# Weight forms of a two-layer MLP made in the first token pass and read back in the second, with VectorE and GpSimd work in another order

## The chip, the cores and the metric

One core of a Trainium2 chip runs the whole program. The metric is the time of one execution in device microseconds, as the median of several runs. A profile of one execution gives the times within it.

## The reference

Of 2048 tokens with 576 features, a spectral filter and then an MLP are computed, each on the layer-normed input and added to it. The biases and scales of the norms are absent.

```python
h  = x + irfft2(rfft2(layernorm(x)) * (w_r + 1j * w_i), s=(2048, 576))
h2 = h + relu(layernorm(h) @ w1) @ w2      # w1: 576 x 4608, w2: 4608 x 576
```

Everything is float32, inputs and output alike.

## The kernel before

**Front part.** The two Fourier transforms are products with constant cosine and sine matrices. The loop over `t` at the end of the listing carries their last stage (`inv_d`, `inv_a`), the second layer norm (`stat2`, `norm2`), and `project`, which transposes the normed tokens for the MLP. Its last seven turns (`t` from 16 to 22) also run block 0 of the MLP.

**Exact products from halves.** TensorE multiplies operands of type fp32r. To keep float32 accuracy each operand v is split in a high half (ScalarE copies v, rounded to fp32r) and a low half (VectorE subtracts the high half from v). A product then is three: high x high, high x low, low x high. `split` does this everywhere. Such a pair of halves is called a form here.

**Seven products for eight.** Both layers use the Strassen-Winograd scheme: of a 2x2 arrangement of blocks seven products are made, from sums of the blocks. The sums on the weights' side are GpSimd's (`sums1` for the first layer: S1 to S4 and one for the rest of 64 features; `sums2` for the second: T1 to T4), the sums on the side of the activations (`hsum`) and the final additions VectorE's.

**Blocks and slots.** The 4608 hidden features are handled as 9 blocks of 512, and the tokens in two passes of 1024: block s = 0 to 8 is the first token pass, s = 9 to 17 the second, with the same weights in the same order (`v % 18`, `s % 9`). A block has two units u = 0 and 1 of 256 hidden features; unit v = 2s + u. A block takes 14 slots k, seven to a unit (m = k % 7). A slot S, k holds on TensorE 6 or 8 matmuls of the first layer for block S (`mm1`, product m) and 12 of the second layer for block S-1 (`prod`, product k of `PRODS`). After the last block there are 14 slots with second-layer products alone. `evac` takes the first layer's result from the PSUM banks X and Y: ScalarE copies X (products 0, 2, 4), VectorE adds Y to such a copy (products 1, 4, 6) into `h`, ScalarE applies relu. Products 1 and 3 both begin in Y, so product 3 waits for the addition of product 1. `form` makes the form of a second-layer operand two slots ahead of its use.

**Order.** Nothing is scheduled automatically: the order in which the Python code issues instructions is each engine's order. In a slot that is `form`, `mm1`, `evac`, `prod` with its addition to the output tile `xs`, then `tasks_old` (work for block S-1) and `tasks_new` (for block S and the next unit). All DMAs of the MLP stand in one queue, SP's; a DMA that waits for a buffer holds back all behind it.

**Weight forms and buffers.** `load1` brings a unit's 576 x 256 weights to one of two buffers `V1`; `sums1` fills `SW` (one buffer); `split1` makes the forms in `WF` in four groups: 0 (A11, A12 and part of the rest; 5 columns of 128), 1 (A22 and rest; 3), 2 (S1, S2; 4), 3 (S3, S4 and the rest's difference; 5). `WF` exists once and a group is overwritten as soon as TensorE has used it. Group 0 is used in products 0 and 1, group 2 in 2 and 3, group 3 in 4 and 6, group 1 in 3 and 5. `load2` brings the second layer's four blocks B11 to B22 to `V2`, T1 to T4 are made in their place or in `T2`, and `split2` makes the seven forms in a ring of four buffers `VF`. `load1`, `load2`, `sums1`, `split1`, `sums2` and `split2` run in each of the 18 blocks.

For the second pass the transposed tokens go through DRAM: `project` writes them to `Td` from seven buffers `h`, and the last seven slots of block 8 read them back into `T` (line 624).

Of the kernel before, what the change touches and what calls it, by code (L numbers as in the profile page):

```python
# [21 lines left out]
NS = 18  # L22
WARM = 60
# [101 lines left out]
def kernel(ctx: ExitStack, tc: tile.TileContext, x, w_r, w_i, w1, w2, cc2, c1, fb, ib, c3, out):  # L125
# [244 lines left out]
    Td = dram.tile([7, 128, 4, 4, 128], F32, tag="Td", name="Td")  # L370
    for k in range(8):
        load_x(xs, 2 * k, 2)
# [52 lines left out]
    def project(i, part):  # L425
# [11 lines left out]
        if P == 0:  # L437
            dsts = [(0, nf, T[:, f0:f0 + nf, :, :, q])]
        else:
            dsts = [(a, b, sb([128, 2, 2, 2, 128], "h", 7, F32R, "mid")[:, :b - a]) for a, b in ((0, 2), (2, nf))]  # L440
        for a, b, dst in dsts:
            act(dst[:, :, 0], pv[:, a:b])
            nc.vector.tensor_sub(dst[:, :, 1], pv[:, a:b], dst[:, :, 0])
        if part == 0:
            rp = pz[64:128, 768:].rearrange("p (c n) -> p c n", c=2)
            act(R[P][64:128, :, q], rp)
            nc.vector.tensor_sub(R[P][0:64, :, q], rp, R[P][64:128, :, q])
        if P:
            for a, b, dst in dsts:
                for f in range(a, b):  # L450
                    nc.sync.dma_start(Td[f0 + f, :, :, i % 4], dst[:, f - a].rearrange("p h k n -> p (h k) n").bitcast(F32))
# [10 lines left out]
    V1, V2, VF, HF, hr = [], {}, [], [], {}  # L462
    M = {}

# [4 lines left out]
    def load1(v):  # L469
        t, f = V1[v % 2], slice(256 * (v % 18), 256 * (v % 18) + 256)  # L470
# [4 lines left out]
    def sums1(v, part, only=None):  # L475
        t, S = V1[v % 2], M["SW"]
# [3 lines left out]
        for n_ in ((0, 1), (2, 3, 4))[part] if only is None else [only]:  # L480
            (nc.gpsimd.tensor_sub if n_ else nc.gpsimd.tensor_add)(*ops[n_])  # L481

    def split1(v, g):
        t, S = V1[v % 2], M["SW"]
        a, b, src = ((0, 5, t[:, :, :128]), (5, 8, t[:, 2:5, 128:]), (8, 12, S[:, 0:4]), (12, 17, S[:, 4:9]))[g]
        split(WF[:, 0, a:b], WF[:, 1, a:b], src)

    def load2(s, n_):
        u, h = int(n_[1]) - 1, int(n_[2]) - 1
        f = 512 * (s % 9) + 256 * u  # L490
        nc.sync.dma_start(V2[n_], w2[f:f + 256, 288 * h:288 * h + 288].rearrange("(j p) d -> p j d", p=128))

    def sums2(*names):
        o = {"T1": ("B11", "B12", "B11"), "T3": ("B12", "B22", "B12"), "T2": ("T2", "B22", "B11"), "T4": ("B21", "B21", "T2")}
        for n_ in names:
            d, a, b = (V2[x] for x in o[n_])
            nc.gpsimd.tensor_sub(d, a, b)  # L497
# [6 lines left out]
    def split2(s, n_):  # L504
        f = vform(s, n_)
        split(f[:, 0], f[:, 1], V2[PLACE.get(n_, n_)])

    def raw(s, q, j=slice(0, 2)):
        if (s, q) not in hr:
            hr[s, q] = sb([128, 2, 512], "h", 7, pool="mid")  # L510
# [44 lines left out]
    def prod(s, k):  # L555
# [6 lines left out]
        for tt in range(2):  # L562
            ops = [(l, r, j) for j in range(2) for l, r in ((0, 0), (0, 1), (1, 0))]
            for n_, (l, r, j) in enumerate(ops):
                nc.tensor.matmul(o[:, tt], f[:, l, j, 128 * tt:128 * tt + 128], w[:, r, j], start=first and n_ == 0,  # L565
                                 stop=n_ == 5, skip_group_check=not first)
        t0 = 8 * (s // 9) + c + 4 * x
# [7 lines left out]
    def tasks_old(s, k):  # L575
        if k == 0:
            hsum(s, "S1", 0)
            hsum(s, "S2", 1)
        if k == 1:
            hsum(s, "S2", 0)  # L580
            split2(s, "T2")
        if k == 2:
            hsum(s, "S4", 0)
        if k == 3:
            split2(s, "T1")
            hsum(s, "S4", 1)
        if k == 4:
            sums2("T4")
        if k == 5:
            split2(s, "B22")  # L590
            split2(s, "T3")
        if k == 8:
            split2(s, "T4")

    def tasks_new(s, k):
        u, m = divmod(k, 7)
        v = 2 * s + u
        if k == 9:
            hsum(s, "S3")
        if k == 11:  # L600
            split2(s, "B11")
            sums2("T1", "T2", "T3")
        if k == 12:
            split2(s, "B21")
        if k == 13:
            hsum(s, "S1", 1)
        if v and k == 7:
            split1(v, 1)
        if v and k in (2, 7):
            split1(v, 3)  # L610
        if m == 0 and v + 2 < 2 * NS:
            load1(v + 2)
        if v + 1 < 2 * NS:
            if v and k in (3, 5, 9, 12):
                sums1(v + 1, int(k in (5, 12)))
            if k in (4, 6, 10, 12, 13):
                split1(v + 1, {4: 0, 6: 2, 10: 0, 12: 2, 13: 1}[k])
        if s:
# [104 lines left out]
```

## Time and profile before

| | |
|---|---|
| median of 3 runs | 1078.07 us (1077.25 to 1078.86) |
| profiled execution | 1077.19 us, span 1075.4 us, granted TensorE clock 0.99 |
| instructions | 16681 |
| block 0 with the last transposes | from about 195 to 240 us |
| blocks 1 to 17 | from about 240 to 1043 us |
| second-layer products alone | from 1043 us |
| DRAM read and written | 71.98 MB and 12.06 MB |

The profile has the columns of the engines: PE is TensorE's matmul, PEld its weight load (which overlaps), DVE VectorE, ACT ScalarE, POOL GpSimd, SP the queue of the DMAs. A row such as `L539 PE MATMUL X<-T,WF` names line, engine, operation, and output and inputs by the program's names; buffer numbers are left out, and `e` is the pool of ten buffers that hold `V1`, `SW`, `V2`, most of `VF` and one of the second-layer operands. `d` are PSUM tiles, `A` is the output tile `xs`, `h` the first layer's result. L467 is the low half in `split`, whichever form it makes, L161 the high half and other ScalarE copies, L516 a sum of activations, L552 the addition of bank Y, L565 the second layer's matmul, L570 the addition to the output, L481 and L497 GpSimd's sums of the first and second layer, L423 its sums for `project`.

### The profile page before, as it was taken

The numbers are of one execution on the slowest core, as the hardware profiler recorded it, in microseconds if no ns is written. First come the engines' busy times: TensorE is split into PE (matmuls) and PEld (weight loads), VectorE is DVE, ScalarE is ACT, GpSimd is POOL, SyncE is SP. The second block draws the span as 40 slices with busy tenths as digits, with TensorE's granted clock in tenths as the row PEclk, the third lists the DMA queues.
The fourth block names the chain that finished last, engine by engine and source line by source line (L and its number), as shares of the span: only waits on it lengthen the run. The fifth ranks groups of instructions, "written<-read, shape, count | busy, mean of one in ns | idle before, by whom it ended". The sixth has DMA issues, their size and how long they took to land.

```text
span 1075.4 us, 16681 instructions
## 1 busy us (share of the span) xinstructions
PE 1011.2 (94%) x6344; PEld 887.4 (83%) x6344; DVE 921.2 (86%) x1367; ACT 514.9 (48%) x904; POOL 368.4 (34%) x384
## 2 busy tenths in 40 slices
PE   8999598779999999999999999999999999999997
PEld 7788476659988988888888989888898988888896
DVE  7587478679899898989989898998989898998987
ACT  4533133556464545545454544545454554545442
POOL 4200166453424252342425235242523424251420
PEclk9999899999999999999999999999999999999999
DMA  8850900563121212112121744212121121212013
GB/s 235 198 133 2 225 1 1 146 183 97 53 67 35 69 36 58 58 44 75 36 69 36 265 147 103 82 36 69 36 58 49 46 82 38 69 30 64 15 31 89
DMA packets 73936, 85.13 MB, mean 79 GB/s; under 512 B 5248, under 2 KB 69248, under 8 KB 72960
## 3 DMA queue, kind: packets, MB, share of 16 engines
q1 hardware_dynamic: 73856, 84.06, 27.7%
q8 instruction: 50, 0.82, 0.3%
q14 instruction: 30, 0.25, 0.1%
HBM read 71.98 MB, written 12.06 MB: 78 GB/s over the span
## 4 chain that ended last, share of the span: by engine, by line
PE 56%; DVE 30%; ACT 7%; issue 3%; DMA 2%; POOL 2%; SPq 1%; POOLq 0%; DVEq 0%; ACTq 0%
PE d L565 22%; PE X L539 15%; PE Y L539 9%; PE d L158 6%; DVE WF L467 6%; DVE e L467 5%; DVE A L570 4%; DVE G L467 3%; DVE h L516 3%; PE dd L158 2%; DVE HF L467 2%; DVE h L552 2%; ACT e L161 1%; ACT WF L161 1%; DVE st L220 1%
## 5 line engine op out<-in xcount | busy, mean ns | idle before, releaser
L539 PE MATMUL X<-T,WF 128*128 128x512 f32 x864 | 230.4, 399 | 12.1 <-DVE WF L467 8.8
L570 DVE TENSOR_TENSOR A<-A,d 128x576 f32<-128x576 f32 x252 | 188.2, 747 | 41.5 <-PE d L565 41.3
L565 PEld LDWEIGHTS d<-e,G 128*128 128x128 f32 x1512 | 213.7, 188 | 11.8 <-issue 1.4
L565 PE MATMUL d<-e,G 128*128 128x288 f32 x1512 | 221.2, 295 | 1.2 <-DVE A L570 1.0
L553 ACT ACTIVATE h<-h 128x512 f32<-128x512 f32 x108 | 68.3, 633 | 315.1 <-DVE h L552 314.7
L481 POOL TENSOR_TENSOR e<-e 128x256 f32<-128x256 f32 (+1 forms) x108 | 98.2, 916 | 300.0 <-DVE WF L467 289.2
L539 PEld LDWEIGHTS X<-T,WF 128*128 128x128 f32 x864 | 154.8, 190 | 44.5 <-DVE WF L467 15.8
L539 PE MATMUL Y<-T,WF 128*128 128x512 f32 x648 | 169.0, 396 | 15.5 <-DVE h L552 15.5
L467 DVE TENSOR_TENSOR WF<-e,WF 128x640 fp32r<-128x640 f32 (+2 forms) x144 | 142.4, 1000 | 32.5 <-ACT WF L161 32.5
L539 PEld LDWEIGHTS Y<-T,WF 128*128 128x128 f32 x648 | 115.4, 188 | 38.6 <-DVE h L552 19.5
L565 PEld LDWEIGHTS d<-e,e 128*128 128x128 f32 x756 | 106.9, 188 | 7.4 <-issue 1.8
L565 PE MATMUL d<-e,e 128*128 128x288 f32 x756 | 110.9, 295 | 1.8 <-DVE A L570 1.6
L565 PEld LDWEIGHTS d<-e,HF 128*128 128x128 f32 x756 | 107.7, 189 | 5.3
L565 PE MATMUL d<-e,HF 128*128 128x288 f32 x756 | 111.2, 296 | 0.0
L497 POOL TENSOR_TENSOR e<-e 128x576 f32<-128x576 f32 x18 | 32.3, 1796 | 229.6 <-DVE e L467 216.9
L467 DVE TENSOR_TENSOR e<-e,e 128x576 fp32r<-128x576 f32 x108 | 96.6, 908 | 15.7 <-ACT e L161 14.4
L516 DVE TENSOR_TENSOR h<-h,h 128x512 f32<-128x512 f32 (+1 forms) x126 | 109.8, 882 | 0.0
L467 DVE TENSOR_TENSOR G<-h,G 128x512 fp32r<-128x512 f32 x126 | 103.6, 823 | 0.1
L161 ACT ACTIVATE WF<-e 128x640 fp32r<-128x640 f32 (+2 forms) x144 | 91.0, 645 | 9.1 <-POOL e L481 9.1
L481 POOL TENSOR_TENSOR e<-e,e 128x256 f32<-128x256 f32 x72 | 82.0, 1139 | 2.8
L161 ACT ACTIVATE u<-X 128x512 f32<-128x512 f32 x72 | 42.5, 590 | 82.4 <-PE X L539 82.3
L161 ACT ACTIVATE G<-h 128x512 fp32r<-128x512 f32 x126 | 77.8, 619 | 6.5 <-DVE h L516 3.5
(103 smaller groups left out, 1296.4 us busy)
## 6 DMA issues: line engine op xcount, KB each, us to landing
e<-in_B_w_dram SPq DMA_DIRECT2D x72, 288.0 KB, 2.9
e<-in_B_w_dram SPq DMA_DIRECT2D x36, 512.0 KB, 3.7
Td<-h SPq DMA_DIRECT2D x28, 256.0 KB, 3.0
T<-Td SPq DMA_DIRECT2D x7, 1024.0 KB, 8.8
A<-in_A_x_dram SPq DMA_DIRECT2D x16, 288.0 KB, 9.2
e<-in_B_w_dram SPq DMA_DIRECT2D x72, 64.0 KB, 3.4
out_dram<-A SPq DMA_DIRECT2D x32, 144.0 KB, 2.5
X<-in_A_x_dram SPq DMA_DIRECT2D x12, 288.0 KB, 7.7
```

The lines of the kernel that those rows point to most:

```text
L158: nc.tensor.matmul(o, l, r, start=start, stop=stop)
L161: nc.scalar.activation(o, i, AF.Copy, **kw)
L220: nc.vector.bn_stats(st[:, i, h, :], xs[:, t0 + i, 288 * h:288 * h + 288])
L467: nc.vector.tensor_sub(l, v, h)
L481: (nc.gpsimd.tensor_sub if n_ else nc.gpsimd.tensor_add)(*ops[n_])
L497: nc.gpsimd.tensor_sub(d, a, b)
L516: f(raw(s, d, j), raw(s, a, j), raw(s, b, j))
L539: nc.tensor.matmul(o, l, r, start=first and n_ == 0, stop=n_ == len(ops) - 1, skip_group_check=not first)
L552: nc.vector.tensor_add(h, a, Y)
L553: nc.scalar.activation(h, h, AF.Relu)
L565: nc.tensor.matmul(o[:, tt], f[:, l, j, 128 * tt:128 * tt + 128], w[:, r, j], start=first and n_ == 0, stop=n_ == 5, skip_group_check=not ...
L570: nc.vector.tensor_add(xt, xt, o)
```

## The change

- Blocks 0 to 9 make the forms as before; block 9, the first of the second pass, works on the same 512 features as block 8, and blocks 10 to 17 on those of blocks 0 to 7 (`fblock`, `made`). In blocks 0 to 7 each form is written to DRAM (`WFd`, `VFd`) right after its split. Blocks 10 to 17 read the forms back into the same places, and have no loads, sums or splits of weights.
- GpSimd's sums stand one to a slot: a unit's five first-layer sums in slots 2 to 6 for the odd unit and 7 to 9, 0, 1 for the even one, T1 to T4 in slots 10 to 13. `SW` has two buffers.
- VectorE's order in a slot is another: `S2` and `S4` are whole sums instead of two halves, the splits of the second layer stand in slots 10, 12, 13 and 3, 4, 5, 7, and the addition to the output (now `total`) comes before the new tasks in odd slots and last in even ones.
- `load1` stands in a unit's third slot instead of its first, and each `load2` right behind the split that frees its buffer.
- `project` writes from four buffers `HF` that later hold the second-layer operands, and issues each write right behind its split. `h` has six buffers.

```diff
-            dsts = [(a, b, sb([128, 2, 2, 2, 128], "h", 7, F32R, "mid")[:, :b - a]) for a, b in ((0, 2), (2, nf))]
+            dsts = [(0, 2, None), (2, nf, None)]
         for a, b, dst in dsts:
+            if P:
+                dst = sb([128, 2, 2, 2, 128], "HF", 4, F32R, "mid")[:, :b - a]
             act(dst[:, :, 0], pv[:, a:b])
             nc.vector.tensor_sub(dst[:, :, 1], pv[:, a:b], dst[:, :, 0])
+            for f in range(a, b) if P else ():
+                nc.sync.dma_start(Td[f0 + f, :, :, i % 4], ...)
...
+    def fblock(s):
+        return s if s < 9 else 8 if s == 9 else s - 10
+
+    def made(s):
+        return s < 10
...
+    GROUPS = ((0, 5), (5, 8), (8, 12), (12, 17))
+
+    def copy1(v, g, back):
+        a, b = GROUPS[g]
+        w, d = WF[:, :, a:b].rearrange("p h a f -> p h (a f)").bitcast(F32), WFd[(v - 20 * back), :, :, 128 * a:128 * b]
+        nc.sync.dma_start(*((w, d) if back else (d, w)))
...
+        if v < 2 * NK1:
+            copy1(v, g, False)
...
+    def copy2(s, n_, back):
+        w, d = vform(s, n_).rearrange("p a j d -> p (a j d)").bitcast(F32), VFd[s - 10 * back, VORDER.index(n_)]
+        nc.sync.dma_start(*((w, d) if back else (d, w)))
...
     def tasks_old(s, k):
         if k == 0:
             hsum(s, "S1", 0)
-            hsum(s, "S2", 1)
         if k == 1:
-            hsum(s, "S2", 0)
-            split2(s, "T2")
+            hsum(s, "S2")
+
+    def tasks_late(s, k):
         if k == 2:
-            hsum(s, "S4", 0)
...
+            hsum(s, "S4")
+        for kk, n_ in ((3, "T1"), (4, "T3"), (5, "B22"), (7, "T4")) if made(s) else ():
+            if k == kk:
+                split2(s, n_)
+        for kk, n_ in ((0, "T1"), (3, "B22"), (4, "T3"), (7, "T4")) if not made(s) else ():
+            if k == kk:
+                copy2(s, n_, True)
...
+        if made(s):
+            if v and m == 0:
+                split1(v, 1)
+            if v and m == 2 - u:
+                split1(v, 3)
+        elif m == 0:
+            copy1(v, 3, True)
...
+            if made((v + 1) // 2):
+                if m == 5 - 2 * u:
+                    split1(v + 1, 0)
+                if m == 6 - 2 * u:
+                    split1(v + 1, 2)
+            else:
+                for mm_, g in ((2, 0), (4, 2), (6, 1)):
+                    if m == mm_:
+                        copy1(v + 1, g, True)
+        if made(s):
+            for kk, n_ in ((10, "B11"), (12, "B21"), (13, "T2")):
+                if k == kk and (s or kk < 13):
+                    split2(s, n_)
+        else:
+            for kk, n_ in ((10, "B11"), (11, "T2"), (12, "B21")):
+                if k == kk:
+                    copy2(s, n_, True)
...
-        if m == 0 and v + 2 < 2 * NS:
+        if 2 <= k < 7 and made(s):
+            sum1(2 * s + 1, k - 2)
+        if 7 <= k < 10 and made(s + 1):
+            sum1(2 * s + 2, k - 7)
+        if k < 2 and s and made(s):
+            sum1(2 * s, k + 3)
+        if m == 2 and made((v + 2) // 2):
             load1(v + 2)
...
+        if made(s):
+            if 10 <= k < 14 and (s or k < 13):
+                sum2("T" + "1234"[k - 10])
+            for kk, n_ in ((4, "B11"), (5, "B12"), (6, "B22"), (8, "B21")) if s else ():
                 if k == kk:
                     load2(s, n_)
...
+            if k % 2:
+                total(S - 1, k)
         if S < NS:
             tasks_new(S, k)
+        if S:
+            tasks_late(S - 1, k)
+            if k % 2 == 0:
+                total(S - 1, k)
```

In the program as built the change shows first on VectorE, which TensorE waits for in slots 3 and 4. These are its instructions from the end of slot 0 to slot 2 in a block of the first pass, before. `HF`, `e<-h` and `G` rows are low halves of second-layer operands, `e<-T` that of T2, the L552 row is the addition that frees Y, and the two `WF` rows are weight groups; the last row is group 3:

```order
L516 TENSOR_TENSOR h_3128<-h_3128,h_3326 128x512
L516 TENSOR_TENSOR h_3047<-h_3128,h_3047 128x512
L467 TENSOR_TENSOR e_2112<-h_3247,e_2112 128x512
L552 TENSOR_TENSOR h_3443<-s_296_1847,Y 128x512
L570 TENSOR_TENSOR A_1284<-A_1284,d_2217 128x2x288
L516 TENSOR_TENSOR h_3047<-h_3128,h_3047 128x512
L467 TENSOR_TENSOR e_2213<-T_300_1857,e_2213 128x576
L467 TENSOR_TENSOR G_2214<-h_3047,G_2214 128x512
L570 TENSOR_TENSOR A_1284<-A_1284,d_2216 128x2x288
L516 TENSOR_TENSOR h_3247<-h_3247,h_3047 128x512
L467 TENSOR_TENSOR WF_1288<-e_1323,WF_1288 128x640
```

The same slots in the change (from slot 0's sum on), where L476 is the low half of `split`, L539 the sum of activations, L575 the addition of Y and L599 the addition to the output:

```order
L539 TENSOR_TENSOR h_3173<-h_3173,h_3383 128x512
L476 TENSOR_TENSOR WF_1288<-e_1321,WF_1288 128x384
L599 TENSOR_TENSOR A_1284<-A_1284,d_2231 128x2x288
L476 TENSOR_TENSOR HF_2175<-h_3295,HF_2175 128x512
L575 TENSOR_TENSOR h_3498<-s_297_1849,Y 128x512
L539 TENSOR_TENSOR h_3089<-h_3173,h_3089 128x1024
L599 TENSOR_TENSOR A_1284<-A_1284,d_2233 128x2x288
L476 TENSOR_TENSOR HF_2229<-h_3089,HF_2229 128x512
L476 TENSOR_TENSOR WF_1288<-e_1325,WF_1288 128x640
L539 TENSOR_TENSOR h_3295<-h_3295,h_3089 128x1024
```

The split of T2 has left the place, the half sums have become one, and the sum S4 stands behind the weight group instead of ahead of it.

The second place is ScalarE at the start of block 1, where the last piece of `project` meets the first second-layer operands. Before (`h_339`, `h_340` are the pieces, `G_343` the operands, `s1` the copy of bank X for product 0):

```order
L161 ACTIVATE h_339_2202<-d_338_2193 128x2x256
L161 ACTIVATE h_340_2203<-d_338_2193 128x2x256
L161 ACTIVATE G_343_2214<-h_302_1887 128x512
L161 ACTIVATE s1_296_1847<-X_1854 128x512
L161 ACTIVATE G_343_2214<-h_326_2074 128x512
```

And now, where `HF_340` and `HF_344` are the same memory, and so are `HF_341` and `HF_345`:

```order
L162 ACTIVATE HF_340_2213<-d_339_2204 128x2x256
L162 ACTIVATE HF_341_2218<-d_339_2204 128x2x256
L162 ACTIVATE e_342_2223<-V_300_1858 128x576
L162 ACTIVATE HF_344_2229<-h_302_1885 128x512
L162 ACTIVATE s1_297_1849<-X_1856 128x512
L162 ACTIVATE WF_202_1288<-e_205_1321 128x384
L162 ACTIVATE HF_345_2230<-h_325_2078 128x512
```

The operand for slot 2 now has to wait until the piece has been written to DRAM, and the copy of bank X stands behind it.

The third place is SP's queue in a block of the first pass. Before it held loads alone (L491 the second layer's, L471 and L473 the first's):

```order
L491 DMA e_1958<-in_B_w_dram 128x2x288
L491 DMA e_1961<-in_B_w_dram 128x2x288
L491 DMA e_1958<-in_B_w_dram 128x2x288
L471 DMA e_1359<-in_B_w_dram 128x4x256
L473 DMA e_1359<-in_B_w_dram 64x256 x2
L491 DMA e_1961<-in_B_w_dram 128x2x288
```

And now (`WFd` and `VFd` are the forms in DRAM, L509 the second layer's loads):

```order
L518 DMA VFd<-e_2223 128x1152
L509 DMA e_1911<-in_B_w_dram 128x2x288
L518 DMA VFd<-e_2121 128x1152
L497 DMA WFd<-WF_1288 256x1x640
L509 DMA e_1911<-in_B_w_dram 128x2x288
L518 DMA VFd<-e_2224 128x1152
L497 DMA WFd<-WF_1288 256x1x512
L509 DMA e_1964<-in_B_w_dram 128x2x288
L497 DMA WFd<-WF_1288 256x1x384
L518 DMA VFd<-e_2173 128x1152
```

The loads of the second layer's weights stand between the copies that write the forms out.

More of the change, by code (lines that the diff above doesn't have):

```diff
@@ L473, in load1, with sum1 @@
             nc.sync.dma_start(t[64 * h:64 * h + 64, 4], w1[512:576, f])
-    def sums1(v, part, only=None):
-        t, S = V1[v % 2], M["SW"]
+    def sum1(v, n_):
+        t, S = V1[v % 2], SW[v % 2]
         A11, A12, A21, A22 = (t[:, 2 * k:2 * k + 2, 128 * f:128 * f + 128] for f, k in ((0, 0), (0, 1), (1, 0), (1, 1)))
```

106 lines of the change are left out of this document (42 added, 64 removed).

## The prediction

> **What bounds the kernel now.** I read the page's busy line first, then a table of stretches of the span, the timeline of TensorE, the chain and the waits. The busy line:
>
> ```profile
> PE 1011.2 (94%) x6344; PEld 887.4 (83%) x6344; DVE 921.2 (86%) x1367; ACT 514.9 (48%) x904; POOL 368.4 (34%) x384
> ```
>
> TensorE and VectorE are both near full, so the share alone doesn't say which one sets the pace. The stretches do (columns: busy time of TensorE, its weight loads, VectorE, ScalarE and GpSimd, then granted clock, DMA share, GB/s):
>
> ```profile
> 250.40:297.00 46.60, 46.60 (x279) 42.32 (x278) 41.54 (x55) 23.42 (x43) 15.96 (x14) 1.00 0.22 66
> ...
> 723.00:770.30 47.30, 45.99 (x268) 40.96 (x268) 42.91 (x57) 23.80 (x43) 16.85 (x14) 1.00 0.18 54
> ...
> 581.10:628.40 47.30, 45.98 (x268) 40.97 (x268) 42.91 (x57) 23.80 (x43) 16.85 (x14) 1.00 0.57 209
> ...
> 1045.00:1075.40 30.40, 22.60 (x158) 21.01 (x156) 24.55 (x38) 10.31 (x18) 0.70 (x1) 0.97 0.33 78
> ```
>
> In the first stretch (block 1) TensorE has no gap at all and its clock is 1.00. In the later blocks about 1.3 us of each 47.30 is a gap. The timeline of TensorE shows where; in brackets stands the idle time before a row and what ended it:
>
> ```profile
> 251.68 1.53 PE L539 MATMUL Y<-T,WF 128*128 128x512 f32 x6
> ...
> 297.86 1.66 PE L539 MATMUL Y<-T,WF 128*128 128x512 f32 x6 [0.86 <-DVE h L552]
> ...
> 723.03 1.66 PE L539 MATMUL Y<-T,WF 128*128 128x512 f32 x6 [0.76 <-DVE h L552]
> ...
> 727.75 1.20 PE L539 MATMUL X<-T,WF 128*128 128x512 f32 x4 [0.55 <-DVE WF L467]
> ...
> 1006.66 1.65 PE L539 MATMUL Y<-T,WF 128*128 128x512 f32 x6 [0.77 <-DVE h L552]
> ...
> 1043.44 3.36 PE L565 MATMUL d<-e,G 128*128 128x288 f32 x24
> ...
> 1050.19 1.83 PE L565 MATMUL d<-e,e 128*128 128x288 f32 x12 [1.63 <-DVE A L570]
> ...
> 1067.31 3.36 PE L565 MATMUL d<-e,G 128*128 128x288 f32 x24
> ```
>
> The same two waits come once in each block: slot 3 waits for VectorE's sum of slot 1 (line 552), which frees bank Y, and slot 4 for the low half of the fourth weight group. The first is the start of a block's slot 3, at 251.68 in block 1 and at 1006.66 in block 17: 754.98 us for 16 blocks, 47.19 us each.
>
> How long would a block take without them? The chain gives the pace of an undisturbed TensorE:
>
> ```profile
> 699.55 1.86 PE Y L539 x8
> 701.40 1.59 PE d L565 x12
> 703.00 1.40 PE X L539 x6
> ```
>
> A block has 14 slots. Eight have 8 matmuls of the first layer (1.86), six have 6 (1.40), and each has 12 of the second (1.59): 14.88 + 8.40 + 22.26 = 45.54 us. Block 1 is a second measure: from 251.68 to 297.86 less the wait of 0.86 and about 0.15 by which a modelled end overstates is 45.17 us. I take 45.4. So TensorE's own floor is 1.8 us below today's pace, and that is nearly all that the steady part has to give.
>
> VectorE is late because GpSimd works in bursts. First rows of VectorE, then of GpSimd, then how far two shapes of VectorE's instruction spread (min/median/max ns):
>
> ```profile
> 711.73 1.92 DVE L467 TENSOR_TENSOR WF<-e,WF 128x512 fp32r<-128x512 f32 x1
> ...
> 717.99 1.92 DVE L467 TENSOR_TENSOR G<-h,G 128x512 fp32r<-128x512 f32 x1
> ...
> 726.88 0.82 DVE L467 TENSOR_TENSOR WF<-e,WF 128x640 fp32r<-128x640 f32 x1
> ```
>
> ```profile
> 707.86 1.82 POOL L497 TENSOR_TENSOR e<-e 128x576 f32<-128x576 f32 x1 [12.71 <-DVE e L467]
> ...
> 711.14 1.95 POOL L497 TENSOR_TENSOR e<-e,e 128x576 f32<-128x576 f32 x1
> ...
> 717.62 1.75 POOL L497 TENSOR_TENSOR e<-e,T 128x576 f32<-128x576 f32 x1
> ```
>
> ```profile
> L467 DVE TENSOR_TENSOR G<-h,G x126: 677/684/1921, 246.2 to 1066.7; 128x512 fp32r<-128x512 f32 x126
> ...
> L570 DVE TENSOR_TENSOR A<-A,d x252: 737/746/756, 246.8 to 1070.7; 128x576 f32<-128x576 f32 x126
> ```
>
> The VectorE instruction begun at 711.73 ends at 713.65, 0.56 after GpSimd's at 713.09; the one at 717.99 ends at 719.91, 0.54 after GpSimd's. A difference of two SBUF operands does nothing until GpSimd's instruction is over, and then takes its usual time. Mean less median over the split and sum groups comes to 5.9 us a block, against 16.85 us of GpSimd work. Eight sums stand in a row from 707.9 to 719.4, just ahead of both late instructions.
>
> **The change, part by part.** *Second token pass (blocks 10 to 17).* Gone are 64 splits of the first layer's weights, 56 of the second's, and 112 GpSimd sums. Rows:
>
> ```profile
> L467 DVE TENSOR_TENSOR WF<-e,WF 128x640 fp32r<-128x640 f32 (+2 forms) x144 | 142.4, 1000 | 32.5 <-ACT WF L161 32.5
> ...
> L467 DVE TENSOR_TENSOR e<-e,e 128x576 fp32r<-128x576 f32 x108 | 96.6, 908 | 15.7 <-ACT e L161 14.4
> ...
> L516 DVE TENSOR_TENSOR h<-h,h 128x512 f32<-128x512 f32 x108 | 87.8, 826 | 0.0
> ...
> L516 DVE TENSOR_TENSOR h<-h,h 128x1024 f32<-128x1024 f32 x18 | 21.9, 1219 | 0.0
> ```
>
> Per block 8 x 1.00 + 7 x 0.908 = 14.4 us leave VectorE, which falls from 42.9 to about 28.5. It can't be late any more; TensorE sets 45.4. Gain 8 x 1.79 = 14.3 us.
>
> In their place SP issues 8 reads of weight forms of layer 1 and 7 of layer 2 a block. WF has one buffer of four groups, so a group is read again only when TensorE has used it. The tightest are the second layer's B21, free at the start of slot 12 and wanted in slot 1 of the next block (3.45 + 3.45 + 2.99 + 1.86 = 11.7 us later), and the groups of A22 and S3/S4, with 12.9. The nearest rows (KB, median us from issue to landing), and what the DMA engines moved from 615 to 650, with the reload of T in its first quarter:
>
> ```profile
> e<-in_B_w_dram SPq DMA_DIRECT2D x36, 512.0 KB, 3.7
> Td<-h SPq DMA_DIRECT2D x28, 256.0 KB, 3.0
> T<-Td SPq DMA_DIRECT2D x7, 1024.0 KB, 8.8
> ```
>
> ```profile
> GB/s 421 440 431 440 421 403 412 421 243 47 4 156 373 214 2 0 0 82 215 50 0 0 0 80 227 153 215 19 0 0 0 22 234 360 58 0 0 36 224 153
> ```
>
> A copy of 0.4 to 0.66 MB therefore lands between 3.0 and 8.8 us after its issue, under 11.7 at either end; I cost it at nothing. 8.6 MB a block in 45.4 us is 190 GB/s, under half of the 421 to 440. The block with the reload (581.10, 209 GB/s, share 0.57) has the same 47.30 us and the same busy times as the others, so traffic doesn't slow the engines.
>
> *First pass (blocks 2 to 9).* All splits and sums stay, 36 pairs of half sums become whole (4 x 0.826 - 2 x 1.219 = 0.87 us less a block), and each form is also written out: 2 x 2.23 + 7 x 0.59 = 8.6 MB more a block in blocks 1 to 7. With today's 2.4 that is 11 MB, 242 GB/s, a good half of what the reload reached. WF groups and second-layer buffers are overwritten five or more slots after the copy is issued, over 15 us against 3.0 to 8.8: nothing. The first layer's loads move from a unit's first slot to its third; they are wanted five slots later (16 us) and land in 3.7. SP used to stand still for the weights of layer 2:
>
> ```profile
> SPq L491 <- DVE e L467: 329.8, 65, 30.2
> ```
>
> Copies behind such a wait would be late, but loads now stand right behind the split that frees their buffer, so the queue follows the program. VectorE's load is 42.0 us of 45.4 if collisions cost what they do now. What counts is that no instruction needed by slots 3 and 4 is behind a burst. T2's split no longer stands ahead of the fourth group's, the pairs of half sums have become whole, and each slot meets one GpSimd instruction. Slots 1 to 3 hold 3.3, 3.5 and 2.2 us without collisions (splits at 0.68 to 0.82, a sum of 1024 columns 1.22, an addition to the output 0.75), 9.0 of TensorE's 9.9, and the split in slot 2 has until slot 4. I leave 0.2 us a block for waits that remain. Gain 8 x 1.59 = 12.7 us.
>
> *End.* Slots 4 to 13 of block 17 lose the second wait, 0.7 us. From 1043.44 the last 14 slots have second-layer matmuls alone: 14 x 1.59 = 22.3 us, yet they end at 1070.67, 27.2 us. VectorE's 24.55 us of the last stretch sheds five splits at 0.68 to 0.76, so TensorE sets the pace: 4.9 us. Together 5.6.
>
> *Start (block 0, with the last transposes).* Today:
>
> ```profile
> 238.92 1.89 PE L434 MATMUL d<-ident,e 128*128 128x128 f32 x6 [4.39 <-POOL e L423]
> 240.46 2.91 PE L539 MATMUL X<-T,WF 128*128 128x512 f32 x6
> 243.16 2.30 PE L565 MATMUL d<-e,HF 128*128 128x288 f32 x12
> ```
>
> ```profile
> 233.48 1.42 POOL L497 TENSOR_TENSOR e<-e 128x576 f32<-128x576 f32 x1 [2.17 <-DVE e L467]
> ...
> 237.69 2.38 POOL L423 TENSOR_TENSOR e<-e,e 128x256 f32<-128x256 f32 x2
> ```
>
> The transposes wait for a GpSimd sum behind three of the second layer's, and after the 4.4 us gap TensorE's next matmuls run at half pace (2.91 for 1.40, 2.30 for 1.59). Now two stand ahead (1.4 us less) and B11, for which the first of them waits, is split a slot earlier (some 2 us), so the gap shrinks by about 3.5 us and the half pace (1.5 + 0.7 us) may go with it: up to 5.7. Against it, HF's four buffers serve the transposed pieces and then the first forms. The third form waits on ScalarE for the last piece's write to land, 3.0 us or more after its split, and the copy of bank X for slot 2 stands behind it: I charge 2.2. Net 3.5, between -3 and 5.7.
>
> **Sum.** 14.3 + 12.7 + 5.6 + 3.5 = 36.1 us. The profiled execution took 1077.19 us (span 1075.4), 0.9 under the median of 1078.07. 1077.19 - 36.1 = 1041.1, so 1041 us.
>
> **A rule beside it.** The Trainium skill, SBUF — State Buffer, section "SBUF: two separate sides", calls the pair of ports that VectorE and GpSimd share "an **exclusive lock**, not a bandwidth split", held for the whole instruction. The two collisions above agree. By it, spreading the sums spares nothing by itself, and if each sum were met in full the first pass would be slower.
>
> **Rivals.** *Collisions grow (ends slower).* In a burst, GpSimd's second sum waits for VectorE too, and only 5.9 of its 16.85 us are lost to VectorE. One sum to a slot could meet VectorE every time. In full that is 42.0 + 10.95 = 52.95 us a block, 5.8 over 47.19: 8 x 5.8 = 46 more, less 14.3, 5.6 and 3.5, gives 1100. Below 11.1 us lost per block the first pass still gains; at 14 (50.1 us a block) the whole comes out level. Against it: a quarter of VectorE's work (14 additions at 0.75 us a block) reads PSUM, and line 570's 252 lie between 737 and 756 ns, so they don't collide. Halfway, with the first pass at its old pace, 12.7 us are lost: 1054.
>
> *The DMA queue bounds the first pass (slower).* 11 MB a block, blocks 1 to 7. It decides where the queue moves under 230 GB/s (47.3 us), and the whole is slower under about 217. Block 0, where most traffic is writing, has the nearest row:
>
> ```profile
> 225.00:239.00 14.00, 8.79 (x41) 6.75 (x42) 8.94 (x12) 9.48 (x18) 7.37 (x7) 0.95 0.63 178
> ```
>
> At 178 GB/s a block would take 62 us: 7 x 14.6 = 102 more, less 25 from the rest: 1154. Against it: the share there was 0.63, so the queue wasn't full, and 209 GB/s took 0.57 above.
>
> *Start gains nothing.* With a DMA queue full of 512-byte pieces the four HF buffers come free late, 3 to 8 us: 1045 to 1050.
>
> *Copies read back late.* If a landing took 15 us, TensorE would wait 3 us in blocks 10 to 17: 1065.
>
> **How the numbers follow.** Floor reached in both passes, 0.72: 1041, from 1033 (floor 45.17, no waits left, start 5.7) to 1050. Collisions that eat the first pass's gain, 0.14: 1050 to 1060. Reading late, 0.05: 1055 to 1070. Start lost, 0.04. Slower through collisions or the queue, 0.05: 1080 to 1155. Range 1031 to 1060, two more below since other waits of block 0 could shorten too. Faster 0.94, same 0.01, slower 0.05, by a bound of 0.2%, about what a measurement of this kernel can tell from no change.
>
> **What would show it.** Right: blocks of 45.2 to 45.6 us in both passes with no wait for the sum of line 552 or for WF; VectorE near 42 us a block, then 28; GpSimd idle from the tenth block on; copies landing within 9 us; the last 14 slots in 22 to 23 us; no half-pace matmuls near 240. Wrong: waits for VectorE in the first pass with long splits beside each sum; a DMA share near 1.0 in blocks 1 to 7; TensorE's weight loads waiting for a DMA in the second pass; ScalarE waiting for the writes of Td in block 1.

## The result and the profile after

The changed kernel takes 1050.34 us (median of four executions, 1047.23 to 1050.98) against 1077.66 for the kernel before: a ratio of 0.9741, 95% interval 0.9718 to 0.9763. The forecast was 1041, with a range from 1031 to 1060. The profiled execution took 1047.23 us (span 1045.5); the other three lie 3 to 4 us above it. The section on the hardware shows one cause of such a difference.

The busy line of the page after:

```profile
PE 1003.4 (96%) x6344; PEld 888.6 (85%) x6344; DVE 784.0 (75%) x1211; ACT 454.2 (43%) x784; POOL 221.1 (21%) x272
```

VectorE has lost 137 us and GpSimd 147; TensorE stands idle for 42 us of the span, where it was 64. Where is read from the stretches, with columns as before. The first row is a block of the first pass, the second one of the second pass, the third the end:

```profile
335.50:382.50 47.00, 46.03 (x269) 40.91 (x269) 41.34 (x55) 23.69 (x44) 15.20 (x14) 1.00 0.65 236
...
753.00:798.50 45.50, 45.50 (x271) 41.40 (x270) 28.25 (x40) 16.31 (x28) 0.00 (x0) 1.00 0.61 191
...
1015.50:1045.50 30.00, 21.45 (x154) 20.38 (x153) 19.23 (x28) 6.10 (x10) 0.00 (x0) 0.97 0.53 151
```

In the second pass TensorE has no gap, VectorE is down to 28 us and GpSimd does nothing. In the first pass about 1 us of gaps is left, and at the end TensorE works 21.45 of 30 us. TensorE's timeline shows the gaps (first pass), and then the starts of block 10 and of block 17:

```profile
429.17 1.65 PE L562 MATMUL Y<-T,WF 128*128 128x512 f32 x6 [0.63 <-DVE h L575]
...
443.41 1.20 PE L562 MATMUL X<-T,WF 128*128 128x512 f32 x4 [0.23 <-DVE WF L476]
...
652.19 1.53 PE L562 MATMUL X<-T,WF 128*128 128x512 f32 x6
...
968.31 1.53 PE L562 MATMUL X<-T,WF 128*128 128x512 f32 x6
```

From 652.19 to 968.31 are 7 blocks of 45.16 us; the copies that they read back land in under 5 us in the median (KB, median us from issue to landing):

```profile
e<-VFd SPq DMA_DIRECT2D x56, 576.0 KB, 4.8
...
WF<-WFd SPq DMA_DIRECT2D x32, 640.0 KB, 4.4
```

In the first pass the wait for bank Y still stands in slot 3. The other has moved from slot 4 to slot 7, and now it is the low half of the first weight group that is late. The gaps in brackets are smaller than the loss, because modelled ends run over: from slot start to slot start, in block 5 slot 2 takes 3.76 us in place of 2.97, slot 3 3.56 in place of 3.42, and slot 7 3.50 in place of 2.97: 1.46 us in all.

The starts of slot 0 in the two timelines divide the whole, in us of the profiled executions:

| stretch | before | after | gain | forecast |
|---|---|---|---|---|
| up to block 1 | 240.46 | 227.70 | 12.76 | start: 3.5 |
| block 1 | 47.03 | 52.82 | -5.79 | (in the start) |
| blocks 2 to 9 | 377.91 | 371.67 | 6.24 | 12.7 |
| blocks 10 to 16, and 17 to its last slot | 374.62 | 357.86 | 16.76 | 14.3 + 0.7 |
| the rest | 35.38 | 35.45 | -0.07 | 4.9 |
| span | 1075.4 | 1045.5 | 29.9 | 36.1 |

Only the second pass came near its forecast. The other three terms are each off by 3.5 to 6.5 us, and they partly cancel. The four places follow.

**Up to block 1.** Most of the gain lies ahead of the places that the prediction looked at. TensorE and GpSimd before, in the inverse transform; then GpSimd after:

```profile
133.77 1.32 PE L158 MATMUL dd<-e,cc 128*128 128x288 f32 x2 [9.77 <-POOL e L396]
```

```profile
131.53 0.72 POOL L481 TENSOR_TENSOR e<-e 128x256 f32<-128x256 f32 x1 [10.80 <-DMA e<-in_B_w_dram]
132.34 0.72 POOL L481 TENSOR_TENSOR e<-e,e 128x256 f32<-128x256 f32 x1
133.02 0.69 POOL L396 TENSOR_TENSOR e<-e 128x287 f32<-128x287 f32 x1
```

```profile
121.78 0.88 POOL L399 TENSOR_TENSOR e<-e 128x287 f32<-128x287 f32 x1 [1.09 <-DVE e L397]
...
132.34 0.72 POOL L490 TENSOR_TENSOR e<-e 128x256 f32<-128x256 f32 x1 [0.47 <-DMA e<-in_B_w_dram]
```

Before, the first weight sum was written at t = 0, ahead of the inverse transform's own subtraction of t = 1 (L396; L399 after). GpSimd takes its instructions in order; the sum waited 10.80 us for a load that landed at 131.5, L396 stood behind it, and TensorE stood behind L396 for 9.77 us. The change writes that sum at t = 4, where the load has all but landed.

The place that the prediction did look at, the gap of 4.39 us near 240, shrank by 2.06 us, to two of 0.99 and 1.34:

```profile
225.12 1.24 PE L437 MATMUL d<-ident,e 128*128 128x128 f32 x6 [0.99 <-POOL e L426]
227.70 2.78 PE L562 MATMUL X<-T,WF 128*128 128x512 f32 x6 [1.34 <-ACT h L571]
```

**Block 1.** What the forecast charged with 2.2 us cost more. ScalarE's and TensorE's rows after:

```profile
237.70 0.63 ACT L162 ACTIVATE HF<-h 128x512 fp32r<-128x512 f32 x1 [2.46 <-DMA Td<-HF]
238.24 0.58 ACT L162 ACTIVATE s<-X 128x512 f32<-128x512 f32 x1
```

```profile
238.87 2.93 PE L562 MATMUL X<-T,WF 128*128 128x512 f32 x6 [2.92 <-ACT s L162]
```

The form of H waits for the write of a transposed piece, the copy of bank X stands behind the form, and TensorE behind the copy, as foreseen. The wait of 2.92 us also left TensorE at half pace, 2.93 us for six matmuls of 1.53.

**First pass.** GpSimd, VectorE and SP around the start of block 5 (slot 0 is at 419.03):

```profile
412.13 1.43 POOL L514 TENSOR_TENSOR e<-e 128x576 f32<-128x576 f32 x1 [17.36 <-DVE e L476]
...
420.48 1.18 POOL L490 TENSOR_TENSOR e<-e,e 128x256 f32<-128x256 f32 x1
...
425.93 0.91 POOL L490 TENSOR_TENSOR e<-e 128x128 f32<-128x128 f32 x1
438.65 0.74 POOL L490 TENSOR_TENSOR e<-e 128x256 f32<-128x256 f32 x1 [11.81 <-DMA e<-in_B_w_dram]
```

```profile
422.94 1.27 DVE L476 TENSOR_TENSOR e<-V,e 128x576 fp32r<-128x576 f32 x1 [0.61 <-ACT e L162]
424.14 1.23 DVE L476 TENSOR_TENSOR HF<-h,HF 128x512 fp32r<-128x512 f32 x1
425.29 1.22 DVE L539 TENSOR_TENSOR h<-h,h 128x512 f32<-128x512 f32 x1
...
428.44 0.68 DVE L575 TENSOR_TENSOR h<-s,Y 128x512 f32<-128x512 f32 x1
```

```profile
427.27 6.21 SPq L497 DMA_DIRECT2D WFd<-WF  x2
433.58 0.56 SPq L481 DMA_DIRECT2D e<-in_B_w_dram  x1
```

The sums are written one to a slot, but nothing holds GpSimd to the slots. It waits for B11's split, then runs eleven sums (four of layer 2, seven of layer 1) from 412.1 to 426.8, those of slots 2 to 6 among them, and then stands still until a load lands. VectorE's splits of 0.68 to 0.75 us and its half sum of 0.68 take 1.22 to 1.27 beside them, just ahead of the sum that frees bank Y (428.44). So the burst has moved, not gone. The low half that slot 7 waits for is made late in the same way: the sums that run once the load has landed (from 438.65) meet the split ahead of it.

```profile
440.69 1.27 DVE L476 TENSOR_TENSOR HF<-h,HF 128x512 fp32r<-128x512 f32 x1
...
442.54 0.81 DVE L476 TENSOR_TENSOR WF<-e,WF 128x640 fp32r<-128x640 f32 x1
```

**The end.** TensorE, then SP:

```profile
1028.35 8.23 PE L588 MATMUL d<-e,HF 128*128 128x288 f32 x60 [2.27 <-DMA e<-VFd]
1037.29 3.43 PE L588 MATMUL d<-e,HF 128*128 128x288 f32 x24 [0.71 <-DMA e<-VFd]
```

```profile
1018.73 5.10 SPq L602 DMA_DIRECT2D out_dram<-A  x4
1023.92 1.03 SPq L518 DMA_DIRECT2D e<-VFd  x2
```

The last 14 slots take 27.2 us as before (1013.5 to 1040.7), but now they wait for read-backs. B22 and T3 are issued at 1023.9, behind four output writes that wait for VectorE's additions.

### The profile page after: what moved, and what is told of

The parts are those of the page before. It is cut to its first block, busy times and chain, and to the rows that moved or that the text cites. A ratio compares the mean times of both kernels' runs of the same rounds, so it can differ in the third digit from the quotient of the medians.

```text
span 1045.5 us, 16643 instructions
## 1 busy us (share of the span) xinstructions
PE 1003.4 (96%) x6344; PEld 888.6 (85%) x6344; DVE 784.0 (75%) x1211; ACT 454.2 (43%) x784; POOL 221.1 (21%) x272
## 4 chain that ended last, share of the span: by engine, by line
PE 58%; DVE 10%; DMA 5%; issue 5%; ACT 3%; SPq 1%; DVEq 0%; ACTq 0%
PE d L588 29%; PE X L562 15%; PE Y L562 14%; DMA e<-in_B_w_dram 3%; DVE WF L476 2%; DVE HF L476 2%; DVE A L599 2%; DVE h L539 1%; DVE h L575 1%; DVE e L476 1%; ACT WF L162 1%; DMA e<-VFd 1%; ACT e L162 1%; DMA Td<-HF 1%; ACT u L162 0%
## 5 line engine op out<-in xcount | busy, mean ns | idle before, releaser
L588 PEld LDWEIGHTS d<-e,HF 128*128 128x128 f32 x3024 | 428.9, 189 | 24.4 <-issue 4.0
L588 PE MATMUL d<-e,HF 128*128 128x288 f32 x3024 | 443.5, 296 | 3.8 <-DMA e<-VFd 3.0
L599 DVE TENSOR_TENSOR A<-A,d 128x576 f32<-128x576 f32 x252 | 188.9, 749 | 111.9 <-PE d L588 111.4
L476 DVE TENSOR_TENSOR HF<-h,HF 128x512 fp32r<-128x512 f32 x252 | 194.7, 773 | 7.8 <-ACT HF L162 6.3
L162 ACT ACTIVATE HF<-h 128x512 fp32r<-128x512 f32 x252 | 156.3, 621 | 31.8 <-PE d L588 15.8
L476 DVE TENSOR_TENSOR WF<-e,WF 128x640 fp32r<-128x640 f32 (+1 forms) x80 | 69.1, 864 | 39.6 <-ACT WF L162 39.6
L539 DVE TENSOR_TENSOR h<-h,h 128x1024 f32<-128x1024 f32 (+1 forms) x90 | 95.2, 1058 | 0.0
L562 PE MATMUL Y<-R,WF 128*128 128x512 f32 x216 | 66.7, 390 | 0.0
L575 DVE TENSOR_TENSOR h<-u,Y 128x512 f32<-128x512 f32 x72 | 49.2, 683 | 17.8 <-ACT u L162 9.7
L476 DVE TENSOR_TENSOR e<-e,e 128x576 fp32r<-128x576 f32 x60 | 46.5, 775 | 13.2 <-ACT e L162 13.2
L162 ACT ACTIVATE WF<-e 128x640 fp32r<-128x640 f32 (+1 forms) x80 | 51.6, 645 | 0.0
L514 POOL TENSOR_TENSOR e<-e 128x576 f32<-128x576 f32 x10 | 14.3, 1434 | 175.1 <-DVE e L476 150.9
```

Of the source, the lines that this page charges most:

```text
L162: nc.scalar.activation(o, i, AF.Copy, **kw)
L476: nc.vector.tensor_sub(l, v, h)
L539: f(raw(s, d, j), raw(s, a, j), raw(s, b, j))
L562: nc.tensor.matmul(o, l, r, start=first and n_ == 0, stop=n_ == len(ops) - 1, skip_group_check=not first)
L575: nc.vector.tensor_add(h, a, Y)
L599: nc.vector.tensor_add(xt, xt, o)
```

## The experiments

Each was run beside the kernel before; medians of four executions, ratios to the kernel before.

**The new order without read-back.** The two DRAM tensors and every copy are gone:

```
 def made(s):
-    return s < 10
+    return s < NS
...
-    if v < 2 * NK1:
-        copy1(v, g, False)
...
-    if s < NK1:
-        copy2(s, n_, False)
```

> All edits of the change stay but one: no weight form is written out or read back, so that the loads, the splits and GpSimd's sums are made in all 18 blocks. Theory A (the read-back frees the second pass, the new order gives the start and about 0.5 us a block, and the copies of the first pass cost nothing): blocks 3 to 8 stay at 46.6 to 46.8 us and blocks 10 to 17 become like them, 8 x 1.5 us more than the changed kernel: 1060 to 1066 us. Rival B (the order freed the second pass too): blocks 10 to 17 at 45.2 us, 1048 to 1052. Rival C (the traffic of the copies is what holds the first pass at 46.7 us): blocks 2 to 9 at 45.2 to 45.6 us, 1038 to 1052.

1058.22 us, ratio 0.9818 (0.9803 to 0.9832). A stretch of 7 blocks of the second pass, from slot 7 of block 10 to slot 7 of block 17:

```profile
674.04:1000.63 326.59, 321.43 (x1878) 286.27 (x1877) 287.31 (x380) 166.02 (x302) 111.99 (x95) 1.00 0.18 53
```

46.66 us a block and 41.0 us of VectorE: the second pass becomes like the first, and theory A holds, if a little under its range. So the read-back is worth 1.2 to 1.5 us a block over the new order alone. Blocks 2 to 9 took 372.19 us without any copies and 371.67 with them: what is written out in the first pass costs nothing that can be seen (two executions of the changed kernel differ by 2.24 us there), though it raises the traffic of blocks 3 to 8 from 75 to 234 GB/s.

**The read-back in the old order.** The kernel before, with copies behind the splits of blocks 1 to 8, and reads in place of loads, sums and splits from block 10 on (the edit in short):

```
+    if 2 <= v < 18:
+        copy1(v, g, False)
...
+    if 1 <= s < 9:
+        copy2(s, n_, False)
...
-    split1(v + 1, ...), split2(s, ...), sums1, sums2, load1, load2
+    copy1(v + 1, g, True), copy2(s, n_, True)      # from block 10 on
```

> The kernel before, in its old order, with the copies alone: forms of blocks 1 to 8 are written out behind their splits, and blocks 10 to 17 read them in place of loads, sums and splits. Theory A: blocks 10 to 17 at 45.2 us in place of 47.3, nothing else moves: 1077.7 - 17 = 1058 to 1064 us. Rival B (without the new order the second pass keeps its waits): 1074 to 1078. Rival C (the copies stand in SP's queue behind the layer-2 loads that wait there, so that splits wait for buffers): blocks 2 to 9 longer than 47.3 us and the time over 1066.

1064.56 us, ratio 0.9874 (0.9859 to 0.9890): A, half a microsecond over its range. Blocks 10 to 16 take 45.45 us each, without the new order; blocks 2 to 9 stay at 378.15 (377.91 before), so no cost of the copies shows here either.

**The front alone.** The kernel before with one edit:

```
-        if t in (0, 1, 4, 5):
-            sums1(t // 4, t % 4)
-        if t in (2, 3, 4):
-            for g in ((2,), (3, 0), (1,))[t - 2]:
+        if t in (4, 5, 8, 9):
+            sums1(t // 4 - 1, t % 4)
+        if t in (6, 7, 8):
+            for g in ((2,), (3, 0), (1,))[t - 6]:
```

> The kernel before with one edit: GpSimd's sums and the splits of the first unit of layer-1 weights come four steps later in the inverse transform, t = 4 to 9 in place of t = 0 to 5. Theory A (the start gained because the sum at t = 0, which waits for a load that lands at 131.5 us, stood in GpSimd's queue ahead of the inverse transform's own work, and TensorE stood still for 9.8 us): that stall goes, and the time falls by 9 to 11 us to 1066 to 1069. Rival B (the start gained by what stands around block 0 - the order of GpSimd's sums, the HF pieces - and the stall at 124 to 134 us is only paid later): 1074 to 1078.

1067.24 us, ratio 0.9899 (0.9883 to 0.9916): A. The wait of 9.77 us has become

```profile
136.35 0.75 PE L158 MATMUL dd<-e,cc 128*128 128x288 f32 x2 [0.74 <-POOL e L396]
```

and all blocks are as before. This edit alone is worth 10.7 us, two fifths of the whole gain.

**GpSimd's sums cut to a column.** The changed kernel, with the same instructions in the same places; the weight sums are therefore not computed:

```
-    (nc.gpsimd.tensor_sub if n_ else nc.gpsimd.tensor_add)(*ops[n_])
+    (nc.gpsimd.tensor_sub if n_ else nc.gpsimd.tensor_add)(*(ops[n_] if v < 2 else (o[..., :1] for o in ops[n_])))
...
-    d, a, b = (V2[x] for x in o[n_])
+    d, a, b = (V2[x][:, :, :288 if s < 1 else 1] for x in o[n_])
```

> The changed kernel, with GpSimd's sums of weights cut to one column from unit 2 and block 1 on, so that order, queues and dependences stay and GpSimd's time nearly goes; the weight sums are therefore not computed. Theory A (the waits left in the first pass come from VectorE's differences that stand still beside GpSimd's sums): blocks 2 to 9 at 45.2 to 45.5 us, 1050 - 11 = 1037 to 1041 us. Rival B (VectorE's own order in slots 0 to 3, with three half sums and a second-layer split ahead of what frees bank Y, makes the wait): blocks stay at 46.2 to 46.7 us, 1046 to 1050.

1038.38 us, ratio 0.9633 (0.9612 to 0.9655): A. Blocks 3 to 8 before, after, and here:

```profile
334.62:618.10 283.48, 275.36 (x1610) 246.03 (x1609) 257.43 (x337) 142.80 (x258) 101.08 (x85) 1.00 0.23 73
```

```profile
325.68:606.19 280.51, 274.97 (x1610) 245.73 (x1609) 246.55 (x324) 142.08 (x258) 92.40 (x85) 1.00 0.65 234
```

```profile
324.11:596.83 272.72, 272.72 (x1610) 245.98 (x1609) 221.76 (x324) 145.05 (x259) 20.61 (x84) 1.00 0.68 241
```

With GpSimd's 15.4 us a block cut to 3.4, VectorE's fall from 41.1 to 37.0, and TensorE has no gap at all (45.45 a block). The waits left in the first pass come from GpSimd's time; VectorE's order alone makes none. In the profile of after no ScalarE copy of a weight is shown waiting for a GpSimd sum, so the sums do not come late; VectorE is slow beside them.

**A later load, to move the sums.** The changed kernel; the second unit's weights are loaded at the block's own slot 0:

```
+        if k == 0 and s and made(s):
+            load1(v + 1)
...
-        if m == 2 and made((v + 2) // 2):
+        if k == 2 and made(s + 1):
             load1(v + 2)
```

> The changed kernel with one edit: in the first pass the layer-1 weights of a block's second unit are loaded at its own slot 0 in place of slot 9 of the block before, so that GpSimd's five sums of that unit cannot run in slots 1 and 2 behind the sums before them. They then stand in slots 3 to 5. Theory A (GpSimd is paced by its inputs, not by the slot that a sum is written in; five sums that meet VectorE in slots 0 to 2 make bank Y late): the 0.8 us before slot 3 goes, what stands before slots 4 and 7 may stay: 0.6 to 1.0 us less a block, 8 x 0.8 = 4 to 8 us less than 1050: 1042 to 1046. Rival B (moved sums cost VectorE as much where they now stand, and the wait moves to slot 7): blocks at 46.4 to 47.0 us, 1048 to 1053.

1044.35 us, ratio 0.9694 (0.9675 to 0.9712): A. GpSimd in block 6, whose slot 3 begins at 471.9; blocks 3 to 8; and the wait that is left in slot 7:

```profile
464.98 0.46 POOL L490 TENSOR_TENSOR e<-e 128x128 f32<-128x128 f32 x1
473.34 0.74 POOL L490 TENSOR_TENSOR e<-e 128x256 f32<-128x256 f32 x1 [7.91 <-DMA e<-in_B_w_dram]
```

```profile
325.66:600.90 275.24, 273.82 (x1610) 245.69 (x1609) 241.59 (x325) 142.09 (x258) 95.71 (x85) 1.00 0.69 243
```

```profile
486.37 1.20 PE L562 MATMUL X<-T,WF 128*128 128x512 f32 x4 [0.54 <-DVE WF L476]
```

The five sums now wait for their load and leave slots 1 and 2 free; the wait for bank Y is gone, and blocks 3 to 8 take 45.9 us, for 46.8. A load's landing paces GpSimd; a place in the program doesn't.

**The order of SP's queue at the end.** The changed kernel, in the last 14 slots:

```
+            for kk, n_ in ((0, "T1"), (2, "B22"), (3, "T3"), (6, "T4")) if S == NS else ():
+                if k == kk:
+                    copy2(S - 1, n_, True)        # ahead of the slot's additions and output writes
...
-            for j in range(2):
-                nc.sync.dma_start(ov[j, :, tiles, d], ...)
+            late.append((tiles, d))               # written from slot 4 on
```

> The changed kernel with one edit in the last 14 slots: the read-backs of B22, T3 and T4 are issued a slot earlier and ahead of the output writes, and the output writes of slots 1 and 3 are held back to slot 4, so that no read-back stands in SP's queue behind a write that waits for VectorE. Theory A (the last 14 slots lost their gain to that queue: the read-back of B22 is issued at 1023.9 us though its buffer is free at about 1018): they take 23.0 to 23.8 us in place of 27.2, and the time falls by 3.4 to 4.2 us, to 1046 or 1047 from 1050. Rival B (ScalarE and VectorE need more than 1.59 us a slot to make the forms of H, whatever the order of the queue): at most 1.5 us less, 1048.5 to 1050.

1045.34 us, ratio 0.9708 (0.9687 to 0.9730): A in its mechanism, and 0.7 us below its range. The wait for a read-back is gone, and the last 14 slots take 23.8 us (1012.5 to 1036.3); the stretch that was 35.45 is 31.92, so 3.5 of the 5.0 us between the medians are shown to lie here:

```profile
1017.87 3.43 PE L589 MATMUL d<-e,HF 128*128 128x288 f32 x24 [0.41 <-ACT HF L162]
1021.67 14.63 PE L589 MATMUL d<-e,HF 128*128 128x288 f32 x108 [0.38 <-issue]
```

**Own buffers for the last pieces.** The changed kernel:

```
+                if (i, part) == (7, 1):
+                    VF.append(ebuf([128, 1152], F32R)...)
+                    dst = VF[-1]...               # first T2 and T1
...
-    split2(0, "T2")                               # end of block 0
...
+        if (s, k) == (0, 1):
+            split2(0, "T2")
```

> The changed kernel with one edit in block 0: the last two transposed pieces that are written to DRAM stand in the two buffers that later hold the first T2 and T1, no longer in the HF ring, and T2's first split moves from the end of block 0 to slot 1 of block 1. Theory A (block 1 takes 52.8 us against 47.0 before because the third form of H waits for the write of those pieces to land): block 1 falls to 46.5 to 48.5 us, the time by 4 to 6 us, to 1044 to 1046 from 1050. Rival B (the wait only moves to T2, whose buffer the same write now holds, or to bank Y): 0 to 2 us less, 1048 to 1050.

1045.09 us, ratio 0.9698 (0.9680 to 0.9717): within A's time, but not by its amount. Block 1 falls to 48.61, 0.1 over what A allows, and two waits stand in it that the profile of after doesn't have there:

```profile
239.55 1.66 PE L566 MATMUL Y<-T,WF 128*128 128x512 f32 x6 [0.33 <-DVE h L579]
...
254.17 1.19 PE L566 MATMUL X<-T,WF 128*128 128x512 f32 x4 [0.55 <-DVE WF L480]
```

Blocks 1 and 2 together take 95.28 us, against 97.98 in the profile of after. The wait for the write is gone, and about half of what block 1 had lost (5.79) with it; VectorE's waits, which it had covered, took the rest. The medians lie 5.25 us apart; the other 2.55 were not located, and TensorE's pace (below) can account for them.

**The changed kernel once more**, unaltered:

> The changed kernel once more, unaltered. Its executions were 1047.2 (profiled) and 1050.3 to 1051.0 (three others). Theory A (an undisturbed TensorE runs at one of two paces, 45.16 or 45.45 us a block, which is set at the last wait and kept to the next): an execution near 1050 has blocks 10 to 16 at 45.45 us, one near 1047 at 45.16, with all else alike within 1 us. Rival B (the 3 us lie in block 0 and block 1, where landing times decide): blocks 10 to 16 at 45.16 us in either, and the difference in the start.

1049.90 us (1048.64 to 1051.18), ratio 0.9747 (0.9727 to 0.9767). The profiled execution took 1051.18; its blocks 10 and 17 start here:

```profile
653.21 1.56 PE L562 MATMUL X<-T,WF 128*128 128x512 f32 x6
...
971.38 1.56 PE L562 MATMUL X<-T,WF 128*128 128x512 f32 x6
```

318.17 us are 45.45 a block, against 45.16 in the execution of 1047.23. Of the 3.9 us between the two spans, 2.05 lie in blocks 10 to 16, where theory A put them. Its claim "all else alike within 1 us" failed: blocks 2 to 9 differ by 2.24, and block 1 by 1.45 the other way.

**Three edits together** (the late load, the end, the own pieces), and **a fourth**, the first group split a slot earlier:

```
-                if m == 5 - 2 * u:
+                if m == 4 - u:
                     split1(v + 1, 0)
```

> The late load, the reordered end and the own pieces in one kernel. Theory (the three places are apart in time, so that their gains add: 5.5 + 4.5 + 4.8 us, less what the pieces give back at the next wait): 1050 - 14 = 1034 to 1038 us. Rival (a wait that ends earlier only lets TensorE reach the next one sooner, so that half of it is lost): 1039 to 1043 us.

> As the kernel with the three edits, and the first group of the second unit's layer-1 weights is split in slot 4 in place of slot 5, ahead of T3's split, so that its low half is made some 3 us earlier. Theory A (the 0.4 to 0.8 us left before slot 8 is that low half alone): the first pass reaches TensorE's own pace, 45.2 to 45.5 us a block, and the time falls 3 to 5 us below the three edits: 1030 to 1034 us. Rival B (VectorE is late as a whole, so that the wait goes to T3, B22 or bank Y): 0 to 1.5 us below the three edits.

Three edits: 1038.10 us, ratio 0.9620 (0.9606 to 0.9635), 0.1 over the theory. Four: 1036.78, ratio 0.9609 (0.9593 to 0.9625), 1.3 us less, as rival B has it. The low half of the first group is in time, and slot 7 waits for the next thing on VectorE instead, B22's low half:

```profile
486.67 1.73 PE L593 MATMUL d<-e,HF 128*128 128x288 f32 x11 [0.21 <-DVE e L481]
```

Blocks 2 to 9 take 367.08 us with three edits and 368.50 with four, so the fourth brought the first pass nothing; its profiled execution ran the second pass at 45.16 a block, that with three at 45.45, so the 1.3 us can't be put down to the edit. Both are faster than the changed kernel (1050.34).

## Why the prediction was right, and where it was not

The time lies in the range, and part of that is luck. The stall at 124 to 134 us was not foreseen, and without the 10.7 us that its removal is worth the time would have been about 1061, over the upper bound of 1060. Two of the signs that the prediction named for being wrong were seen: waits for VectorE in the first pass with long splits beside the sums, and ScalarE waiting for the writes of Td in block 1.

- **Second pass: right.** 16.76 us against 15.0. The old pace of 47.2, TensorE's own 45.4 (measured 45.16 or 45.45), 28 us of VectorE, and copies that land in time were all as said, and the read-back alone brings the pace. "Copies read back late" came true only at the end, where they were issued late and not slow to land.
- **Copies of the first pass at nothing: right** within some 2 us over the pass, in two pairs of kernels. The rival in which the DMA queue bounds the first pass is out.
- **First pass: the size was wrong, 6.24 for 12.7.** The step that failed is "each slot meets one GpSimd instruction". It read the program's order as time. An engine that waits only for its operands runs ahead of the slots, and eleven sums still stood in a row. The load counted was right (42.0 us of VectorE forecast, 41.1 measured) and under TensorE's pace, but a mean over a block does not say whether bank Y is freed in time. The rival "collisions grow" was wrong in sign: VectorE loses some 4.1 us a block to them, and the estimate for before was 5.9. Half of the gain came, which lies between the forecast and the rival's "halfway", where all 12.7 us were lost. Which part of the new order brought the 6.24 was not taken apart. (The burst of before, called eight sums, has nine in the timeline; nothing hangs on it.)
- **The loads "are wanted five slots later (16 us) and land in 3.7": wrong.** They stood in SP's queue behind copies that wait for their splits (the row of 6.21 us at 427.27), and GpSimd waited 11.81 us for one. That kept three sums out of the slots ahead of bank Y, but put them ahead of the low half that slot 7 waits for.
- **End: 4.9 us forecast, none measured.** "TensorE sets the pace" left out that a slot there is 1.59 us, so that a read-back of 4.8 us takes three of the four slots between the release of B22's buffer and its use, and that SP's queue holds output writes ahead of it. VectorE's limit was lifted, and the queue took its place.
- **Start: 6.97 net against 3.5, for other reasons.** With the front edit alone block 1 begins at 231.39, 9.07 us earlier than before: that is the stall of 9.77 us at 124 to 134, which lies ahead of every stretch that the prediction read. The other 3.69 us up to block 1 come from around block 0. The forecast had 3.5 there from the gap near 240 alone; that gap gave 2.06, the rest was not taken apart, and the half pace did not go with it (2.78 us for six matmuls at 227.70). The charge of 2.2 us for the pieces had the right mechanism and too small a price: block 1 lost 5.79, half pace included.

With 6.5 and 4.9 us too much, and 1.8 and 3.5 too little, the sum was 6.2 us too high against the profiled execution. The rest to the median, 3.1 us, is what the profiled execution lies below it.

## What to carry to other kernels

Read the whole timeline of the engine that bounds for its largest gap before working on the regular ones, and ask of every instruction that is moved what stands behind it in its own queue. An instruction's place in the program fixes what it follows on its own engine, not the slot of another engine beside which it runs: to keep an engine's work out of a crowded stretch, make its input land later. Where a bound is lifted, look at the shortest slots for what is late next, and at every in-order queue for a wait that does not concern the transfers behind it.

## What the runs showed of the hardware

**Two paces of TensorE.** With the granted clock at 1.00 and no gap, a block takes 45.16 us in some stretches and 45.45 in others, six matmuls of 512 columns 1.53 or 1.56. Each of the nine profiles with read-back keeps one of the two over all of blocks 10 to 16: four at 45.16 (the execution of 1047.23 us among them), five at 45.45 (that of 1051.18). The pace can change at a wait, as in block 9 of the execution of 1047.23:

```profile
606.19 1.56 PE L562 MATMUL X<-T,WF 128*128 128x512 f32 x6
...
616.24 1.66 PE L562 MATMUL Y<-T,WF 128*128 128x512 f32 x6 [0.49 <-DVE h L575]
...
619.79 1.53 PE L562 MATMUL X<-T,WF 128*128 128x512 f32 x6
```

Over 17 blocks this is 4.9 us, about the spread of the kernel with the cut sums, which has no wait after block 1 (1035.41 to 1040.50). What sets the pace was not found, and an edit worth less than 5 us here is read by its stretches, not by one execution.

**The clock after a gap.** The same place in two executions of the changed kernel, after a gap of 2.92 and of 2.94 us:

```profile
239.00:241.50 2.50, 2.50 (x6) 2.02 (x7) 2.50 (x6) 0.86 (x2) 0.00 (x0) 0.50 0.59 234
```

```profile
239.00:241.50 2.50, 2.39 (x13) 2.14 (x14) 2.50 (x5) 1.10 (x3) 0.00 (x0) 1.00 0.65 253
```

In the first the granted clock is 0.50, in the second 1.00, and block 1 took 52.82 and 51.37 us. The Trainium skill, TensorE: Matmul & The Clock Gate, Part 1 (the HAM clock gate), says that the window over which activity is judged is free-running; that nearly the same gap has either outcome agrees with it. The page puts that window at about 3.4 us, and here a gap of 2.92 us was enough: the measurement decides.
